# Query tiles in three buffers, a block's two averages in one place, and products in single PSUM banks, in a two-layer linear-attention kernel on one core

## The chip, the cores and the metric

The kernel runs on one NeuronCore of a Trainium2 chip. A core has TensorE (PE in the profile; its weight loads are PEld), VectorE (DVE), ScalarE (ACT), GpSimd (POOL) and SyncE (SP, which here issues the DMAs). Each takes its own instructions in order, and they wait for each other through semaphores. Matmuls write PSUM, which ScalarE and VectorE read. PSUM has eight banks; a tile of 512 float32 columns on 128 partitions fills one.

The metric is the device time of one execution in microseconds, the median of several. What matters for a change of well under one per cent is the median beside the spread of the runs.

## The reference

There are two layers with the same weights, and each is an attention half and a dense half. With S = 2048 rows, D = 640, H = 32 heads of Dh = 20 and F = 1536:

```python
q, k, v = split(layernorm(x) @ wqkv)                 # per head, Dh = 20
phi_q = concat([softmax(q @ w_phi), softmax(-(q @ w_phi))])   # 2 * Dh features
phi_k = concat([softmax(k @ w_phi), softmax(-(k @ w_phi))])
kv = phi_k^T v ;  z = sum over rows of phi_k         # over all S rows
o  = (phi_q kv) / (phi_q z + 1e-6)
x  = x + o @ wo
x  = x + mish(layernorm(x) @ w1 + b1) @ w2
```

The sums `kv` and `z` run over all rows. So no row's average `o` can be formed until the last key has been summed.

## The kernel before

**Tiling.** The 2048 rows are eight blocks (`NB`) of 256 rows, each two tiles (`BT`) of 128. All products of activations and weights are done as three matmuls in a split format: a high part by a high part, high by low, low by high. A product of 640 input columns therefore takes 5 x 3 = 15 matmuls for one half of the output columns (`project_half`, L354), and 30 for both (`project`). Transposed input comes as three pieces per block, of 2, 2 and 1 chunks of 128 columns; ScalarE makes the high part of each (`xth`) and VectorE the low part (`xtl`, L296).

**First stage of attention, `attend_first`.** For each block the kernel projects keys, values and queries of both tiles, in the order k0 k1 v0 v1 q0 q1 in most blocks. `features` then turns a projected tile into 1280 features: ScalarE copies the two PSUM halves into an SBUF tile `e` of 128 x 1280 (through the helper at L122), VectorE takes maxima and minima (L384) and the differences (L385, L387; for queries GpSimd does L385), ScalarE does the exponential, VectorE the sums (L393) and reciprocals (L394), GpSimd the product (L395). A key tile is then multiplied with the values into the running sum `kva` (L430), both tiles of a block one after the other, during the next block. A query tile is transposed in place by VectorE (L439) and stored by four DMAs (L443) to the DRAM tensor `e_d` of its block.

The tile `e` of a key is a `big_tile`, a pool with five buffers. The tile of query `i` is `query_tile(i)` (L368): one of two fixed SBUF tiles, `r210` and `r211` (both shown as `r` in the profile), that hold weights in the dense half. The PSUM pairs that the projections use are `mm_tile`, two buffers of two banks each. The other four banks are `one_tile`, four buffers of one bank each.

In this stage a scheduler orders each engine's instructions. In layer 0 it starts behind the folding of weights, in layer 1 behind the last steps of the dense half.

**Second stage, `attend_second`.** For TensorE and SP the order is the one that is written down. `load(b)` reads a block's query features back, transposed: two big tiles (L548) and a small one (L549). `load(0)` is called in the last block of the first stage; `load(1)` is called behind the last products of that stage, `load(2)` and `load(3)` after the averages that precede the block loop, and `load(b + 3)` inside it. `average(b, t)` multiplies the features of tile t with the block-diagonal sums `kvb` (L589, 44 matmuls as the trace counts them) into an `mm_tile`. VectorE divides by the denominators with five operations (L598, L599, L602) into a row tile. The division is `div[0]`, behind which `tail()` places one more step of what is left over from the first stage (`rest`: the second query tile of the last block, and the stores of that block's queries).

In each block b of the loop, the rows of block b are multiplied with `wo` (`Rows.half`, 15 matmuls each for two tiles and two column halves). VectorE adds each product to the residual (L619) and takes statistics (L620, L624). Between them stand the averages of block b + 1 and its transposes (L290, ten as the trace counts them). The second tile's two products go into the two banks of one `mm_tile`, `py`; the first tile's go into one bank each. SP's issues in a block are the next rows of x (L400), `load(b + 3)`, the store of the block (L671) and weights for the dense half (L147).

The dense half that follows (L697, L739) is not touched.

Of the kernel before, what the change touches and what calls it, by code (L numbers as in the profile page):

```python
# [8 lines left out]
F32 = mybir.dt.float32  # L9
# [17 lines left out]
NB = S // BLK  # L27
# [21 lines left out]
def kernel(  # L49
# [22 lines left out]
    def mm_tile():  # L72
        return psum.tile([P, 2, 512], F32, tag="mm", name="mm", bufs=2)

    def one_tile():
        return psum.tile([P, 512], F32, tag="one", name="one", bufs=4)

    def big_tile():
        return work.tile([P, EW], F32, tag="big", name="big", bufs=5)
# [7 lines left out]
    def row_block(t, b):  # L87
        return t[b * BLK:(b + 1) * BLK, :].rearrange("(p t) d -> p t d", t=BT)
# [75 lines left out]
    def r2_wide(j, dtype=F32R):  # L164
        return wts.tile([P, 2, D], dtype, tag=f"r2{j}", name=f"r2{j}")
# [140 lines left out]
    def row_tile():  # L306
        return work.tile([P, D], F32, tag="xn", name="xn", bufs=4)
# [40 lines left out]
    def project_half(ps, xts, t, ws, col, c, ks=range(KD), w=HC):  # L348
        sl = slice(t * P, (t + 1) * P)
        cs = slice(col + c * w, col + (c + 1) * w)  # L350
        for k in ks:
            h, l, wh, wl = xts.hs[k], xts.ls[k], ws[k][0][:, cs], ws[k][1][:, cs]
            for n, (a, r) in enumerate(((h, wh), (h, wl), (l, wh))):
                nc.tensor.matmul(ps[:, :w], a[:, sl], r, start=(k == 0 and n == 0),  # L354
                                 stop=(k == KD - 1 and n == 2))
# [9 lines left out]
        return g % 4, 2 * DH * (3 * (g // 4) + j)  # L365

    def query_tile(i):
        return r2_wide(10 + i % 2, F32).rearrange("p s d -> p (s d)")  # L368

    def features(ps, e, pool_sub):  # L370

# [26 lines left out]
    def fetch(x_src, b, xt=None):  # L398
        xt = x_tile() if xt is None else xt
        nc.sync.dma_start(xt, row_block(x_src, b))  # L400
        return xt
# [139 lines left out]
    def load(b):  # L541

        ta, tb, tc_ = big_tile(), big_tile(), pair_tile(F32)
        for t, g0 in ((ta, 0), (tb, 5)):

            src = e_d[b][120 * g0:120 * (g0 + 4) + P]
            src = bass.AP(tensor=src.tensor, offset=src.offset, ap=[[BLK, P], [120 * BLK, 5], [1, BLK]])
            nc.sync.dma_start(t.rearrange("f (g s) -> f g s", s=BLK), src)  # L548
        nc.sync.dma_start(tc_[:80, 0], e_d[b][1200:])  # L549
        return [(ta, tb)[g // 5][:, (g % 5) * BLK:(g % 5 + 1) * BLK] for g in range(10)] + [tc_[:, 0]]  # L550

    def finish_kv(kva):

        acc = row_tile()
        nc.vector.tensor_copy(acc[:, :360], kva[:, :360])
        yield
        ps = one_tile().rearrange("p (n q c) -> p n q c", n=4, c=32)
        for n in range(3):
            nc.tensor.transpose(ps[:120, n], acc[:, 120 * n:120 * (n + 1)], ident)
        for n, q, r, w in ((0, 4, 120, 3), (1, 4, 120, 3), (2, 2, 120, 3), (2, 1, 80, 2)):  # L560
            g = 4 * n + (2 if w == 2 else 0)
            q0 = 2 if w == 2 else 0
            nc.vector.tensor_tensor(
                kvb[:r, g:g + q, :(DH + 1) * w].rearrange("f q (j c) -> f q j c", j=w),
                ps[:r, n, q0:q0 + q, :DH + 1].unsqueeze(2).to_broadcast([r, q, w, DH + 1]),
                mask[:r, :w].unsqueeze(1).unsqueeze(3).to_broadcast([r, q, w, DH + 1]), op=ALU.mult)
        yield

    def attend_second(x_src, x_dst, acc, fetches, makes, fetch_next, begin_next):
        kva, o_ws, loaded, rest = acc  # L570
        rows = {}
        div = [None]

        def tail():

            with tc.issue_after(div[0]):
                next(rest, None)

        def average(b, t):

            phs = loaded[b]
            po = mm_tile()
            for g in range(G):
                n = 120 if g < 10 else 80
                w = GW if g < 10 else 42
                c, j = divmod(g, 8)
                for q in range(2):
                    s0 = t * P + 64 * q
                    nc.tensor.matmul(  # L589
                        po[64 * q:64 * q + 64, c, GW * j:GW * j + w], phs[g][:n, s0:s0 + 64],  # L590
                        kvb[:n, g, :w], start=True, stop=True)
            o = row_tile()
            den = work.tile([P, H], F32, tag="r", name="den", bufs=2)
            pv = [po[:, c, :(DH + 1) * n].rearrange("p (h d) -> p h d", d=DH + 1)
                  for c, n in ((0, 24), (1, 8))]
            hh = (slice(0, 24), slice(24, H))
            for c in range(2):
                nc.vector.tensor_scalar_add(den[:, hh[c]], pv[c][:, :, DH], DEN_EPS)  # L598
            nc.vector.reciprocal(den, den)  # L599
            for c in range(2):  # L600
                n = hh[c].stop - hh[c].start
                ins = nc.vector.tensor_tensor(o.rearrange("p (h d) -> p h d", d=DH)[:, hh[c]], pv[c][:, :, :DH],  # L602
                                        den[:, hh[c]].unsqueeze(2).to_broadcast([P, n, DH]), op=ALU.mult)
                div[0] = ins.ins
            rows.setdefault(b, []).append(o)
            if t == BT - 1:
                del loaded[b]

        class Rows:


            def __init__(self, b, t):
                self.t, self.xt, self.ps = t, xs[b], None
                self.bn = work.tile([P, 2, 6], F32, tag="bn", name="bn", bufs=2)

            def half(self, c, ps):
                project_half(ps, cur, self.t, o_ws, 0, c)
                part = self.xt[:, self.t, c * HC:(c + 1) * HC]
                nc.vector.tensor_tensor(part, ps[:, :HC], part, op=ALU.add)  # L619
                nc.vector.bn_stats(self.bn[:, c], part)  # L620

            def mean(self):
                mv = work.tile([P, 2], F32, tag="mv", name="mv", bufs=3)
                nc.vector.bn_aggr(mv, self.bn)  # L624
                return mv

        with tc.manual_schedule(engines={mybir.EngineType.PE, mybir.EngineType.SP}):
            kv = finish_kv(kva)
            next(rest)
            next(kv)  # L630
            loaded[1] = load(1)
            xs = {0: fetch(x_src, 0)}
            fetches[0]()
            next(rest)
            next(kv)
            next(rest)
            average(0, 0)
            average(0, 1)
            loaded[2] = load(2)
            average(1, 0)  # L640
            cur = Transposed(rows.pop(0)).all()
            average(1, 1)
            loaded[3] = load(3)
            for b in range(NB):
                if b == NB - 1:
                    ahead.all()
                elif b:
                    average(b + 1, 0)
                r0, r1 = Rows(b, 0), Rows(b, 1)
                r0.half(0, one_tile())  # L650
                if 0 < b < NB - 1:
                    average(b + 1, 1)
                tail()
                if b + 1 < NB:
                    xs[b + 1] = fetch(x_src, b + 1)
                if 0 < b and b + 3 < NB:
                    loaded[b + 3] = load(b + 3)
                if b == NB - 3:
                    fetch_next()
                r0.half(1, one_tile())  # L660
                mv0 = r0.mean()
                if b == NB - 2:
                    ahead = begin_next()
                py = mm_tile()
                r1.half(0, py[:, 0])
                if b + 1 < NB:
                    nxt = Transposed(rows.pop(b + 1)).all()
                r1.half(1, py[:, 1])
                norm_scale(b, [mv0, r1.mean()])
                xt = xs.pop(b)  # L670
                nc.sync.dma_start(row_block(x_dst, b), xt)  # L671
                makes[b]()
                if b + 1 < NB:
                    fetches[b + 1]()
                tail()
                if b < NB - 1:
                    cur = nxt
            for _ in rest:
                pass
        return ahead  # L680
# [217 lines left out]
```

## Time and profile before

| | |
|---|---|
| runs | 1399.83, 1400.14, 1402.13 us |
| median | 1400.14 us |
| the profiled execution | 1399.85 us, of which the span of the trace is 1397.9 us |
| mean granted TensorE clock | 0.994 |
| TensorE busy | 1364.9 us, 98% of the span |
| VectorE, ScalarE, GpSimd busy | 1089.6, 587.7 and 460.1 us |
| attention, layer 0 | about 18 to 350 us |
| attention, layer 1 | about 715 to 1055 us |

A row of the timeline gives start, duration, engine, line, operation, what it writes and reads, its size, how many such instructions were merged, and in brackets the idle time of the engine before it with what ended it. A row of the waits gives who waited for whom, the total in us, the number of waits and the longest. `L354` is line 354 of the kernel. Buffer numbers are left out of tile names, so `big` is any of the five big buffers, and `r` is either query tile (and the small tile of sums).

### The profile page before, as it was taken

The page shows a single profiled execution, that of the slowest core. Times are in us where ns is not written, and L with a number is a line of the kernel's source. Part 1 is how long each engine was busy: PE and PEld are TensorE (multiplying, and loading weights), DVE is VectorE, ACT ScalarE, POOL GpSimd, SP SyncE. Part 2 cuts the span into 40 slices and gives each one's busy share as a digit, 9 for nine tenths or more (in the row PEclk, how much of TensorE's full clock was granted, in tenths as well). Part 3 has the DMA queues.
Part 4 walks back from the last instruction along what each step waited for, and adds up shares of the span by engine and source line. Part 5 has one row for each costly group of instructions (what it writes and reads, how often), then busy time and mean ns, then how long its engine had stood idle before and what let it go on. Part 6 is the DMA issues. An engine that isn't in the chain of part 4 may idle for free. (4 is left out here: it accounts for less than half of the span.)

```text
span 1397.9 us, 30903 instructions
## 1 busy us (share of the span) xinstructions
PE 1364.9 (98%) x12866; PEld 1345.4 (96%) x12866; DVE 1089.6 (78%) x1814; ACT 587.7 (42%) x1035; POOL 460.1 (33%) x344
## 2 busy tenths in 40 slices
PE   7999999999999999999999999999999999999998
PEld 7989999999999999999999999989999999999998
DVE  5798877886688887788769899988667766777775
ACT  4444434222445454545443343432134544444443
POOL 1443543353442222222234544453344211211112
PEclk9999999999999999999999999999999999999999
DMA  8532434788624432344472433458965212333200
GB/s 312 156 60 63 88 51 93 201 242 290 207 62 95 114 96 65 73 107 104 137 229 56 91 67 58 67 118 268 279 236 177 74 26 71 95 95 95 68 28 20
DMA packets 350277, 169.03 MB, mean 121 GB/s; under 512 B 287097, under 2 KB 323689, under 8 KB 350137
## 3 DMA queue, kind: packets, MB, share of 16 engines
q1 hardware_dynamic: 350137, 167.06, 44.4%
q8 instruction: 101, 1.65, 0.5%
q14 instruction: 39, 0.32, 0.1%
HBM read 104.43 MB, written 62.59 MB: 119 GB/s over the span
## 5 line engine op out<-in xcount | busy, mean ns | idle before, releaser
L739 PE MATMUL mm<-r2h,ol 128*128 128x320 f32 x1280 | 305.4, 309 | 1.4 <-ACT ol L722 0.9
L723 POOL TENSOR_TENSOR ol<-big,ol 128x512 fp32r<-128x512 f32 (+1 forms) x98 | 130.6, 1333 | 458.1 <-ACT ol L722 393.0
L697 PE MATMUL one<-xtl,r1h 128*128 128x256 f32 x960 | 268.6, 280 | 2.0 <-DVE xtl L296 2.0
L697 PE MATMUL one<-xth,r1l 128*128 128x256 f32 x960 | 268.0, 279 | 0.0
L697 PE MATMUL one<-xth,r1h 128*128 128x256 f32 x960 | 266.5, 279 | 0.0
L739 PEld LDWEIGHTS mm<-r2h,ol 128*128 128x128 f32 x1280 | 219.1, 188 | 2.8 <-POOL ol L723 1.5
L739 PE MATMUL mm<-r2l,ol 128*128 128x320 f32 x640 | 197.3, 309 | 0.0
L354 PE MATMUL mm<-r1h,xth 128*128 128x304 f32 (+1 forms) x600 | 186.7, 311 | 6.8 <-ACT r L122 6.8
L354 PE MATMUL mm<-r1h,xtl 128*128 128x304 f32 (+1 forms) x600 | 185.4, 309 | 2.3 <-DVE xtl L296 2.2
L354 PE MATMUL mm<-r1l,xth 128*128 128x304 f32 (+1 forms) x600 | 185.5, 309 | 0.0
L697 PEld LDWEIGHTS one<-xtl,r1h 128*128 128x128 f32 x960 | 180.4, 188 | 2.7 <-DVE xtl L296 2.5
L697 PEld LDWEIGHTS one<-xth,r1l 128*128 128x128 f32 x960 | 180.4, 188 | 0.0
L697 PEld LDWEIGHTS one<-xth,r1h 128*128 128x128 f32 x960 | 179.9, 188 | 0.0
L712 DVE TENSOR_SCALAR big<-big 128x512 f32<-128x512 f32 (+1 forms) x98 | 56.6, 578 | 112.9 <-ACT big L710 112.9
L354 PE MATMUL mm<-r2h,xth 128*128 128x304 f32 (+1 forms) x460 | 142.6, 310 | 0.0
L354 PE MATMUL mm<-r2h,xtl 128*128 128x304 f32 (+1 forms) x460 | 140.4, 305 | 0.0
L354 PE MATMUL mm<-r2l,xth 128*128 128x304 f32 (+1 forms) x460 | 140.2, 305 | 0.0
L395 POOL TENSOR_TENSOR r<-r,r 128x1280 f32<-128x1280 f32 x32 | 77.5, 2423 | 149.0 <-DVE r L394 126.7
L354 PEld LDWEIGHTS mm<-r1h,xth 128*128 128x128 f32 x600 | 114.0, 190 | 8.1 <-ACT r L122 7.3
L710 ACT ACTIVATE big<-one,b1s 128x256 f32<-128x256 f32 x192 | 80.6, 468 | 96.2 <-PE one L697 95.6
L714 ACT ACTIVATE big<-big,two 128x512 f32<-128x512 f32 (+1 forms) x98 | 70.1, 715 | 119.2 <-DVE big L713 116.7
L739 PEld LDWEIGHTS mm<-r2l,ol 128*128 128x128 f32 x640 | 120.2, 188 | 0.0
(130 smaller groups left out, 3031.6 us busy)
## 6 DMA issues: line engine op xcount, KB each, us to landing
e_d<-r SPq DMA_DIRECT2D x128, 160.0 KB, 4.0
big<-e_d SPq DMA_DIRECT2D x32, 640.0 KB, 7.3
x_d<-xt SPq DMA_DIRECT2D x23, 640.0 KB, 4.0
xt<-x_d SPq DMA_DIRECT2D x22, 640.0 KB, 4.9
n_d<-xn SPq DMA_DIRECT2D x176, 80.0 KB, 2.4
xt<-in_x SPq DMA_DIRECT2D x16, 640.0 KB, 5.1
xn<-x_d SPq DMA_DIRECT2D x28, 320.0 KB, 4.2
v<-n_d SPq DMA_DIRECT2D x30, 256.0 KB, 3.2
```

What stands on the lines that cost most here:

```text
L354: nc.tensor.matmul(ps[:, :w], a[:, sl], r, start=(k == 0 and n == 0), stop=(k == KD - 1 and n == 2))
L395: nc.gpsimd.tensor_tensor(eg, eg, r.unsqueeze(2).to_broadcast([P, 2 * H, DH]), op=ALU.mult)
L697: nc.tensor.matmul(ph[:, j, :], l, r, start=(n == 0), stop=(n == 3 * KD - 1))
L710: exps[0] = nc.scalar.activation(part(ta, 0)[:, j - js.start], ph[:, j, :], AF.Exp, bias=b1s[:, 2 * pr + j:2 * pr + j + 1]).ins
L712: nc.vector.tensor_scalar_min(e, e, E_CAP)
L714: nc.scalar.activation(r, n, AF.Ln, bias=two)
L723: nc.gpsimd.tensor_tensor(al[:, js], n, ah[:, js].bitcast(F32), op=ALU.subtract)
L739: nc.tensor.matmul(pys[t][:, c, :HC], l[:, j, sl], r, start=(f == 0 and n == 0), stop=(f == KF - 1 and n == 2))
```

## The change

Three edits, all in the attention half.

```diff
     def query_tile(i):
-        return r2_wide(10 + i % 2, F32).rearrange("p s d -> p (s d)")
+        return big_tile() if i % 3 == 2 else r2_wide(10 + i % 3, F32).rearrange("p s d -> p (s d)")
```

Queries 0, 3, 6, 9, 12 and 15 use `r210`, queries 1, 4, 7, 10 and 13 use `r211`, and queries 2, 5, 8, 11 and 14 take one of the five buffers of the pool that keys and loads use. The number of big buffers stays five.

```diff
                 elif b:
                     average(b + 1, 0)
+                    average(b + 1, 1)
                 r0, r1 = Rows(b, 0), Rows(b, 1)
                 r0.half(0, one_tile())
-                if 0 < b < NB - 1:
-                    average(b + 1, 1)
                 tail()
```

In blocks 1 to 6 the second tile's average moves ahead of the first product with `wo`. `tail()` stays behind that product.

```diff
-                py = mm_tile()
-                r1.half(0, py[:, 0])
+                r1.half(0, one_tile())
                 if b + 1 < NB:
                     nxt = Transposed(rows.pop(b + 1)).all()
-                r1.half(1, py[:, 1])
+                r1.half(1, one_tile())
```

In every block the second tile's two products each take a single bank from the four. A block's turns in those banks become seven (four products, three transposes) instead of five, and its turns in the pairs two instead of three.

## The prediction

> **What bounds the kernel now.** I read the page first, then who waits for whom on TensorE, then the same question for ScalarE and VectorE in layer 1's first attention stage (735 to 945 us), and last the granted clock around TensorE's long waits.
>
> ```profile
> span 1397.9 us, 30903 instructions
> PE 1364.9 (98%) x12866; PEld 1345.4 (96%) x12866; DVE 1089.6 (78%) x1814; ACT 587.7 (42%) x1035; POOL 460.1 (33%) x344
> ```
> ```profile
> PE mm L354 <- ACT r L122: 6.8, 2, 3.8
> PE mm L589 <- PE mm L589: 0.9, 2, 0.4
> ```
> ```profile
> ACT r L122 <- DMA e_d<-r: 54.5, 12, 8.9
> DVE m L384 <- ACT r L122: 14.0, 7, 3.1
> ```
>
> TensorE is busy for 1364.9 of 1397.9 us, so an edit is worth what it removes from the 33 us that are left, or what it saves between matmuls. TensorE's largest wait is 6.8 us in two pieces: a projection needs a PSUM pair that ScalarE has not emptied. The fifth row says why: ScalarE cannot copy a query product into its SBUF tile, because that tile's predecessor is still being stored to `e_d`, 54.5 us of waiting in 12 pieces. VectorE in turn idles 14.0 us for those copies (775 to 945 us).
>
> ```profile
> 89.74 0.68 ACT L122 ACTIVATE r<-mm 128x608 f32<-128x608 f32 x1 [10.14 <-DMA e_d<-r]
> 90.47 0.41 PE L354 MATMUL mm<-r1h,xth 128*128 128x304 f32 x1 [3.03 <-ACT r L122]
> 770.00 0.68 ACT L122 ACTIVATE r<-mm 128x608 f32<-128x608 f32 x1 [8.91 <-DMA e_d<-r]
> 770.73 0.54 PE L354 MATMUL mm<-r1h,xth 128*128 128x304 f32 x1 [3.77 <-ACT r L122]
> 858.39 0.41 PE L354 MATMUL mm<-r1h,xtl 128*128 128x304 f32 x1 [1.83 <-DVE xtl L296]
> ```
> ```profile
> 770.85:774.26 3.41, 3.41 (x14) 3.41 (x15) 2.48 (x3) 0.25 (x1) 3.41 (x2) 0.50 0.92 143
> 856.18:859.59 3.41, 1.58 (x11) 1.33 (x10) 2.15 (x3) 0.32 (x1) 3.29 (x2) 1.00 0.85 145
> 859.60:863.01 3.41, 3.41 (x82) 3.11 (x84) 2.88 (x4) 1.33 (x4) 1.27 (x1) 0.50 0.23 79
> ```
> ```profile
> 961.86 2.20 PE mm L354 x15
> ```
>
> In the stretches (start:end, length, busy time of PE, PEld, DVE, ACT and POOL, granted clock, DMA share, GB/s) the clock is 0.50 for 3.41 us after such a wait. In one of them TensorE starts 14 matmuls; at full clock 15 take 2.20 us, about 0.145 each, so 3.41 us would fit 23 or 24. Each drop thus costs some 1.4 us on top of its wait. A wait of 1.83 us has already brought one on.
>
> **First edit: a third query tile.** With three buffers the copy of query i waits for the store of query i-3 instead of i-2. It is worth something different at each place.
>
> *Layer 0, at 90 us.* Query 3's tile becomes that of query 0, stored long before, so ScalarE's 10.14 us go. But VectorE is full here (61.8 of 63 us):
>
> ```profile
> 51.40:114.40 63.00, 59.97 (x643) 58.26 (x642) 61.84 (x75) 29.31 (x48) 30.84 (x21) 0.97 0.37 77
> ```
> ```profile
> 87.71 0.76 DVE L387 TENSOR_TENSOR big<-m,big 128x640 f32<-128x640 f32 x1
> 91.16 1.47 DVE L384 TENSOR_REDUCE m<-r 128x32 f32<-128x640 f32 x2
> ```
> ```profile
> 90.43 1.26 ACT L122 ACTIVATE big<-big 128x1280 f32<-128x1280 f32 x1
> 91.60 0.37 ACT L122 ACTIVATE xth<-one 128x256 fp32r<-128x256 f32 x1
> ```
>
> In the changed program's order query 3's reductions (1.47 us) stand ahead of the key's subtraction (87.71, 0.76 us), and ScalarE does that key's exponential (1.26 us) before the next block's last transposed piece (0.37 us). So the subtraction ends near 87.7 + 1.5 + 0.8 = 90.0, the exponential near 91.2, the piece near 91.6. TensorE starts that block at 87.4 (90.47 less the wait), runs the 12 matmuls that need no such piece, and waits from 89.1 to 91.6: 2.5 us, and the clock drops again. What is left is a head start of 12 matmuls (1.7 us) less what the key sums, split differently behind it, take of that: I take **0.4 us**, near the low end, because VectorE's row is full; bounds 0 and 3.03 + 1.4 = 4.4.
>
> *Layer 1, at 770 us.* Query 2 is copied at once, but VectorE is late with the next block's low parts:
>
> ```profile
> 767.90 0.62 DVE L296 TENSOR_TENSOR xtl<-xn,xth 128x512 fp32r<-128x512 f32 x1
> 770.86 1.55 DVE L384 TENSOR_REDUCE m<-r 128x32 f32<-128x640 f32 x2 [1.88 <-ACT r L122]
> 772.33 1.02 DVE L296 TENSOR_TENSOR xtl<-xn,xth 128x256 fp32r<-128x256 f32 x1
> ```
>
> The key projection can start at 767.0 (770.73 less the wait). It waits some 0.5 us for the second low part (ends 768.5) and 1.5 to 2 us for the third, which stands behind a reciprocal (0.5 us) and the reductions (1.55) and itself takes up to 1.02 us: 771 to 771.5. By the row at 858 that drops the clock too. The projection's end moves from 776.5 to about 775: **1.5 us**; bounds 0 and 3.77 + 1.4 = 5.2.
>
> *Layer 1, at 858 us.* The low part that TensorE lacks stands on VectorE behind a query's reductions, which wait for the query's copy, which waits for a store. Here VectorE has room:
>
> ```profile
> 776.00:942.00 166.00, 160.91 (x1882) 158.24 (x1884) 151.31 (x159) 64.68 (x110) 75.01 (x37) 0.99 0.41 77
> ```
>
> It is busy 151.3 of 166 us, and nearly all of the rest is the 14.0 us for the copies. The stall goes with its drop: 1.83 + 1.4 = **3.2 us**; bounds 0 and 3.2.
>
> *Layer 1, the key sums that end the stage.*
>
> ```profile
> ACT r L122 <- DMA e_d<-r: 8.4, 2, 4.5
> ```
> ```profile
> 260.12 1.48 PE L430 MATMUL one<-big,v 128*21 128x40 f32 x128 [0.68 <-POOL big L395]
> 941.08 2.26 PE L430 MATMUL one<-big,v 128*21 128x40 f32 x128 [3.18 <-POOL big L395]
> 916.89 0.82 DVE L384 TENSOR_REDUCE m<-r 128x32 f32<-128x640 f32 x1 [2.16 <-ACT r L122]
> ```
>
> In layer 0 (first row, 110 to 262 us) only two copies wait for stores, and the sums wait 0.68 us. In layer 1 they wait 3.18 us with a dropped clock, at the end of work that VectorE began 2.16 us late at 916.89, for a query's copy. I expect layer 0's wait: 2.5 + 1.4 = **3.9 us**; bounds 0 and 4.6.
>
> By the Trainium skill (TensorE: Matmul & The Clock Gate, "What's actually happening") the clock falls only after an idle window of about 3.4 us; by that the split waits at 90 and 770 us would keep it, and those two terms would come out at 1.8 and 2.9 us. The trace differs: 1.83 us of idle time in the window that ends at 859.59 was enough.
>
> **Its price in the big buffers.** The five now also hold queries 2, 5, 8, 11 and 14.
>
> ```profile
> 736.96 0.66 ACT L122 ACTIVATE r<-mm 128x608 f32<-128x608 f32 x1
> ```
> ```profile
> 230.65 9.71 SPq L548 DMA_DIRECT2D big<-e_d  x3
> 261.02 0.38 SPq L548 DMA_DIRECT2D big<-e_d  x1
> ```
> ```profile
> 267.36 0.80 PE L589 MATMUL mm<-kvb,big 120*64 120x63 f32 x20 [0.43 <-PE mm L589]
> 268.41 0.80 PE L589 MATMUL mm<-kvb,big 120*64 120x63 f32 x20 [0.24 <-DMA big<-e_d]
> ```
> ```profile
> 266.90:270.30 3.40, 2.72 (x56) 2.54 (x54) 2.64 (x11) 0.37 (x1) 0.00 (x0) 1.00 1.03 378
> ```
>
> Six blocks fill the 166 us above, 27.7 us each; eight tiles in three blocks leave each 52 us. A query needs 33 (copied at 736.96, stored by 770.00), a key about as long. No price there. It comes at the end of the stage: query 14 holds a fifth buffer until its last store, so `load(1)` has no free buffer and waits for the last keys' sums. Before, three halves of the first two loads were issued from 230.65 on; the fourth, issued at 261.02, landed at 268.4, just in time. Now the third goes at about 261.0 and the fourth when the sums end, at 261.6. Behind them on SP stand the rest of the load, x, a weight and the next load, all needed several us later. The DMA engines are full (share 1.03), so 640 KB more at 378 GB/s are 1.7 us. Block 1's first average begins at 268.4 instead of 267.36 and its second half between 269.2 and 270.1 instead of 268.41: 0.8 to 1.7 us, plus about a third of a chance of a drop. I take **+1.8 us per layer, +3.6**; bounds per layer 0 (layer 1 had slack) and 6, if the second half is 4.5 us late and the clock drops.
>
> **Second edit: averages together.** 44 matmuls (L589) move ahead of 15, in blocks 1 to 6 of each layer, with five VectorE operations and no DMA.
>
> ```profile
> 946.70 2.72 PE mm L589 x88
> ...
> 964.06 1.41 PE mm L589 x44
> 965.47 2.40 PE one L354 x15
> ...
> 973.89 1.09 PE one L290 x10
> ...
> 977.18 1.41 PE mm L589 x44
> ```
>
> 15 matmuls behind an average take 2.40 us, elsewhere 2.20. The block is 977.18 - 964.06 = 13.12 us; together it is 2.72 + 2.40 + 3 x 2.20 + 1.09 = 12.81. Twelve times 0.31 = **3.7 us**; bounds 0 and 3.7. The first product's addition on VectorE comes 1.4 us later; its bank is next needed two products on.
>
> **Third edit: single banks.** No matmul changes, and the pair that it frees has no waiter inside the blocks (the 0.9 us lie ahead of them). The last product reuses the third one's bank, emptied by L619 while ten transposes run (1.09 us):
>
> ```profile
> 987.04 0.49 DVE L619 TENSOR_TENSOR xt<-mm,xt 128x320 f32<-128x320 f32 x1 [0.94 <-PE mm L354]
> ```
>
> That leaves 0.6 us of cover. If L619 came late by one more 0.5 us operation, nothing would show; by two, some 0.4 us in 14 places, 5.6. VectorE was waiting here, so I take 0.
>
> **The sum.** -0.4 - 1.5 - 3.2 - 3.9 + 3.6 - 3.7 = -9.1 us on the profiled execution's own 1399.85 us (span 1397.9), 0.3 below the median of 1400.14: **1391 us**, own range 1386 to 1396.
>
> **Rivals.**
> *The waits vanish altogether.* For it: the copies' wait is the named releaser in every case. Against: VectorE is full at both early places. With the clock kept at 90 and 770 us and at the loads: -1.8 - 2.9 - 3.2 - 3.9 - 3.7 + 2.6 = -12.9, **1387**; with every upper bound and no price, 1379. The skill's clock rule points here.
> *VectorE stays behind.* The stalls at 858 and 941 us come back with VectorE as releaser. For it: 91% busy. Against: its 14.0 us of idle time. -0.4 - 1.5 - 3.7 + 3.6 = -2.0, **1398**.
> *The late load decides, slower.* Both halves of `load(1)` queue in the full DMA stretch, land 4.5 us late and drop the clock, 6 us per layer, with VectorE behind as well: -5.6 + 12 = +6.4, **1406**. It decides from 2.8 us per layer on. For it: share 1.03 and 0.24 us of slack; against: the full stretch moves 640 KB in 1.7 us.
> *The third tile changes nothing*, the store of query i-3 being late too: -3.7 + 3.6, **1400**.
>
> **How the numbers follow.** Forecast 0.50, waits vanish 0.17, VectorE behind 0.18, late load 0.12, nothing 0.03. A measurement tells 0.2% (2.8 us) from no change; a third of "VectorE behind" gets that far. Faster 0.72, same 0.16, slower 0.12. The range, 1382 to 1401, leaves out the late load and the far end of the first rival.
>
> **What would show it.** Right: no TensorE wait on ScalarE's `r`; short waits on transposed pieces near 89 and 768 us in their place; none near 855; layer 1's key sums waiting under 1 us; L589 in groups of 88 of some 2.7 us; 1 to 2 us of DMA wait at block 1's first average. Wrong: key copies waiting for a big buffer, or a load wait above 3 us.

## The result and the profile after

The changed kernel takes 1388.55 us, median of four runs (1387.53 to 1390.38), against 1399.99 us (1398.67 to 1402.13) for the kernel before on the same chip. The ratio is 0.9918, with a 95% interval of 0.99 to 0.9936: faster, as forecast, and 2.4 us below the 1391 of the forecast. The profiled execution took 1389.55 us.

The page of the changed kernel, span and engines:

```profile
span 1387.5 us, 30850 instructions
PE 1359.7 (98%) x12866; PEld 1342.9 (97%) x12866; DVE 1080.9 (78%) x1814; ACT 587.3 (42%) x1035; POOL 461.0 (33%) x344
```

Who waits for whom on TensorE in the changed kernel (total us, number, longest):

```profile
PE mm L354 <- DVE xtl L296: 3.0, 4, 1.4
PE mm L354 <- ACT xth L122: 2.7, 1, 2.7
...
PE mm L589 <- DMA big<-e_d: 1.1, 1, 1.1
```

The largest row of before, 6.8 us on ScalarE's `r`, is gone. The same view for ScalarE (735 to 945 us) and for VectorE (770 to 940 us):

```profile
ACT r L122 <- DMA e_d<-r: 6.0, 1, 6.0
```
```profile
DVE m L384 <- ACT r L122: 2.6, 3, 0.9
```

Of ScalarE's 54.5 us of waiting for stores 6.0 are left, of VectorE's 14.0 us for query copies (775 to 945 us) 2.6. So the third tile took the copies' waits away. TensorE's waits that remain, from the timeline of the changed kernel:

```profile
91.99 0.48 PE L354 MATMUL mm<-r1h,xth 128*128 128x304 f32 x1 [2.66 <-ACT xth L122]
...
94.13 0.62 PE L354 MATMUL mm<-r1h,xtl 128*128 128x304 f32 x1 [0.74 <-DVE xtl L296]
...
269.08 0.80 PE L589 MATMUL mm<-kvb,big 120*64 120x63 f32 x20 [0.43 <-DVE xn L602]
270.98 0.80 PE L589 MATMUL mm<-kvb,big 120*64 120x63 f32 x20 [1.10 <-DMA big<-e_d]
...
769.05 0.41 PE L354 MATMUL mm<-r1h,xtl 128*128 128x304 f32 x1 [0.51 <-DVE xtl L296]
...
771.55 0.62 PE L354 MATMUL mm<-r1h,xtl 128*128 128x304 f32 x1 [1.39 <-DVE xtl L296]
...
933.36 1.48 PE L430 MATMUL one<-big,v 128*21 128x40 f32 x128 [0.94 <-POOL big L395]
```

Nothing waits near 855 us. Layer 1's key sums wait 0.94 us instead of 3.18. The waits at 92 and 770 us changed their releaser: ScalarE's and VectorE's own order in place of a store. Around them, in stretches of the granted clock (start:end, length, busy time of PE, PEld, DVE, ACT and POOL, granted clock, DMA share, GB/s):

```profile
88.77:92.18 3.41, 0.75 (x6) 0.50 (x5) 3.41 (x4) 1.78 (x3) 3.41 (x2) 1.00 0.09 25
92.19:95.60 3.41, 2.67 (x38) 2.19 (x38) 3.38 (x7) 0.50 (x2) 2.78 (x2) 0.50 0.00 0
95.60:99.01 3.41, 3.41 (x43) 3.11 (x44) 1.91 (x2) 0.42 (x1) 2.73 (x2) 0.50 0.15 25
768.03:771.44 3.41, 1.62 (x10) 1.12 (x8) 3.41 (x7) 0.83 (x2) 2.84 (x2) 1.00 0.92 143
771.44:774.85 3.41, 3.30 (x13) 3.30 (x14) 3.41 (x4) 0.00 (x0) 3.41 (x2) 0.50 0.88 154
```

In layer 0 the clock is at half for two windows now, where it was one; at 771 us still for one; at 860 and 941 us no longer.

The averages stand together (timeline of the changed kernel; 40 and 4 matmuls are one average):

```profile
952.17 1.25 PE L290 MATMUL one<-ident,xn 128*128 128x128 f32 x10
...
955.55 1.38 PE L589 MATMUL mm<-kvb,big 120*64 120x63 f32 x40
...
958.25 0.42 PE L354 MATMUL one<-r2h,xth 128*128 128x320 f32 x1
...
990.53 1.25 PE L290 MATMUL one<-ident,xn 128*128 128x128 f32 x10
```

Both take 2.70 us (955.55 to 958.25), and three blocks 38.36 us (952.17 to 990.53): 12.79 each, where before a block took 13.12.

Four stretches sort the gain and all the experiments: A from layer 0's first key sums (L430) to its last group of them, B from there to the third contraction of the dense half (its 49th matmul of L739 before, L737 after; 11.3 us behind the first in every run), C and D the same in layer 1. "Half" is the time at half clock ahead of the last few us. A to D and "half" are of one profiled execution, the median is of all runs.

| kernel | A | B | C | D | half | median us |
|---|---|---|---|---|---|---|
| before | 183.87 | 136.94 | 189.33 | 138.02 | 13.7 | 1400.1 |
| changed | 185.37 | 135.79 | 181.14 | 135.27 | 10.2 | 1388.55 |
| changed, again (e8) | 185.22 | 135.54 | 180.37 | 134.97 | 6.8 | 1388.48 (one run) |
| e1 third tile alone | 185.93 | 138.34 | 180.37 | 138.16 | 6.8 | 1394.39 |
| e2 averages alone | 182.20 | 135.47 | 189.73 | 136.65 | 10.2 | 1397.05 |
| e3 banks alone | 183.67 | 136.48 | 189.52 | 138.83 | 13.7 | 1399.20 |
| e4 third tile in layer 1 | 182.18 | 134.47 | 180.36 | 136.26 | 0 | 1385.27 |
| e5 query 14 apart | 184.96 | 134.50 | 181.19 | 135.77 | 10.2 | 1388.02 |
| e6 early piece | 179.87 | 135.54 | 181.29 | 135.66 | 0 | 1384.45 |
| e7 = e5 + e6 | 179.87 | 134.47 | 181.33 | 135.59 | 0 | 1383.78 |
| e9 early in layer 0 | 179.86 | 134.47 | 180.38 | 135.94 | 0 | 1382.78 |
| e10 early in both | 179.98 | 134.60 | 179.82 | 134.78 | 0 | 1381.35 |

The whole gain of the change lies in C (-8.2), D (-2.75) and B (-1.15). A became longer by 1.5 us.

### The profile page after: what moved, and what is told of

Its sections match the earlier page's. It is cut to its first block, busy times and chain, and to the rows that moved or that the text cites. A ratio compares the mean times of both kernels' runs of the same rounds, so it can differ in the third digit from the quotient of the medians.

```text
span 1387.5 us, 30850 instructions
## 1 busy us (share of the span) xinstructions
PE 1359.7 (98%) x12866; PEld 1342.9 (97%) x12866; DVE 1080.9 (78%) x1814; ACT 587.3 (42%) x1035; POOL 461.0 (33%) x344
## 4 chain that ended last, share of the span: by engine, by line
PE 80%; DVE 7%; DMA 2%; ACT 1%; issue 1%; POOL 1%; DVEq 0%; ACTq 0%; POOLq 0%; SPq 0%
PE one L695 22%; PE mm L737 21%; PE mm L354 20%; PE one L354 11%; PE mm L589 3%; PE one L290 2%; PE one L430 1%; DVE m L384 1%; DVE r L393 1%; DVE xtl L296 1%; DVE big L710 1%; DVE big L717 1%; DMA big<-e_d 1%; DVE r L439 1%; DVE big L711 0%
## 5 line engine op out<-in xcount | busy, mean ns | idle before, releaser
L737 PE MATMUL mm<-r2h,ol 128*128 128x320 f32 x1280 | 305.4, 310 | 1.5 <-ACT ol L720 0.9
L737 PEld LDWEIGHTS mm<-r2h,ol 128*128 128x128 f32 x1280 | 219.2, 188 | 2.8 <-POOL ol L721 1.5
L737 PE MATMUL mm<-r2l,ol 128*128 128x320 f32 x640 | 197.4, 309 | 0.0
L395 POOL TENSOR_TENSOR big<-big,r 128x1280 f32<-128x1280 f32 x42 | 102.7, 2444 | 82.5 <-DVE r L394 66.6
L737 PEld LDWEIGHTS mm<-r2l,ol 128*128 128x128 f32 x640 | 120.3, 188 | 0.0
L354 PEld LDWEIGHTS mm<-r1h,xtl 128*128 128x128 f32 x600 | 114.3, 191 | 4.0 <-DVE xtl L296 4.0
L720 ACT ACTIVATE ol<-big 128x512 fp32r<-128x512 f32 (+1 forms) x98 | 61.0, 622 | 131.4 <-DVE big L719 131.3
L354 PEld LDWEIGHTS mm<-r1l,xth 128*128 128x128 f32 x600 | 114.2, 190 | 0.2
```

The source lines that it names most:

```text
L395: nc.gpsimd.tensor_tensor(eg, eg, r.unsqueeze(2).to_broadcast([P, 2 * H, DH]), op=ALU.mult)
L720: nc.scalar.activation(ah[:, js], n, AF.Copy)
L737: nc.tensor.matmul(pys[t][:, c, :HC], l[:, j, sl], r, start=(f == 0 and n == 0), stop=(f == KF - 1 and n == 2))
```

## Experiments

All edits are on the changed kernel unless "before" is named. The kernel before ran beside each group of them, at 1400.1 us.

### e1, e2, e3: the three edits one at a time (on the kernel before)

```diff
# e1
-        return r2_wide(10 + i % 2, F32)...
+        return big_tile() if i % 3 == 2 else r2_wide(10 + i % 3, F32)...
# e2
                     average(b + 1, 0)
+                    average(b + 1, 1)
...
-                if 0 < b < NB - 1:
-                    average(b + 1, 1)
# e3
-                py = mm_tile()
-                r1.half(0, py[:, 0])
+                r1.half(0, one_tile())
...
-                r1.half(1, py[:, 1])
+                r1.half(1, one_tile())
```

> The kernel before with the third query tile alone. Theory (the waits for the stores were the larger part, the averages the smaller, and the two add up): the change's 11.4 us less 12 x 0.33 for the averages leaves -7.4 us on 1400.0, 1392.6; no TensorE wait on ScalarE's r, layer 1's key sums near 933.5 us, blocks of the second stage still 13.1 us each. Rival (the gain of layer 1 needs the averages or the banks too, which leave the pair free earlier): -4 us or less, 1396 to 1400. Rival (the third tile is all of it): -11, 1389.

Measured: 1394.39 us, ratio 0.996 (0.9947 to 0.9972), -5.7 us. The theory holds for C, which is as short as with all three edits (180.37), and for the waits on `r`, which are gone. It was 1.8 us too hopeful. Two of TensorE's three waits for `e_d` (timeline of e1) show where:

```profile
269.82 0.80 PE L589 MATMUL mm<-kvb,big 120*64 120x63 f32 x20 [1.18 <-DMA big<-e_d]
...
271.53 0.80 PE L589 MATMUL mm<-kvb,big 120*64 120x63 f32 x20 [0.91 <-DMA big<-e_d]
```

2.09 us where the kernel before waited 0.43 + 0.24. B is 1.4 us longer than before. So the third tile is about half of the gain, and the rival that it is all of it falls.

> The kernel before with a block's two averages in one place, second tile's products still in a pair. Theory: 12 blocks of about 12.79 instead of 13.12 us, -4.0 us on 1400.0, 1396.0; first stages as before. Rival (the averages' saving needs the single banks, since average, average and product pair take turns in two pairs): 0 to -1 us, 1399 to 1400, with waits of TensorE on VectorE's additions (L619) ahead of L589 or L354.

Measured: 1397.05 us, ratio 0.9978 (0.997 to 0.9987), -3.1 us, between the two. Blocks 1 and 2 of the loop take 13.32 and 13.15 us, the other four 12.79, in both layers. TensorE's waits in e2, 270 to 395 us, and the two places in its timeline:

```profile
PE mm L589 <- DVE xt L619: 0.5, 2, 0.3
```
```profile
281.40 0.80 PE L589 MATMUL mm<-kvb,big 120*64 120x63 f32 x20 [0.33 <-DVE xt L619]
...
294.55 0.63 PE L589 MATMUL mm<-kvb,big 120*64 120x63 f32 x14 [0.17 <-DVE xt L619]
```

An average needs the pair that the second tile's products have just filled, and VectorE has not emptied it. That costs 0.53 + 0.36 = 0.9 us a layer, 1.8 in all; why blocks 3 to 6 don't wait stays open. So the second edit is worth its 0.33 us in every block only with the third. A is 1.7 us shorter than before, which is not the edit's: e3 and e2 both wait 2.85 us for the store near 90 us (the kernel before 3.03), but in e2 no half clock follows (windows of e3, then of e2):

```profile
87.63:91.04 3.41, 1.26 (x9) 1.26 (x10) 3.41 (x5) 1.99 (x4) 2.72 (x2) 1.00 0.22 43
91.04:94.45 3.41, 3.41 (x65) 3.00 (x65) 3.38 (x6) 1.00 (x3) 3.41 (x2) 0.50 0.00 0
```
```profile
88.16:91.57 3.41, 1.63 (x11) 1.63 (x12) 3.41 (x5) 2.36 (x5) 2.72 (x2) 1.00 0.08 24
```

A of e3 and A of e2 (183.67 and 182.20) thus price one window of half clock at 1.5 us; the forecast had 1.4.

> The kernel before with the second tile's products in single banks alone. Theory: no difference beyond 0.5 us, 1400; blocks still 13.12 us. Rival (the last product waits for L619's addition to empty the third one's bank): +0.4 us in 14 places, 1405.6. Rival (the pair was a hidden wait): blocks shorter by 0.1 us and more, 1398 or less.

Measured: 1399.2 us, ratio 0.9995 (0.9986 to 1.0004): no difference. Blocks take 13.12 us. Both rivals fall. Alone the banks are worth nothing; they keep the averages' gain whole.

### e4: the third tile in layer 1 only

```diff
-        return big_tile() if i % 3 == 2 else r2_wide(10 + i % 3, F32)...
+        if layer:
+            return big_tile() if i % 3 == 2 else r2_wide(10 + i % 3, F32)...
+        return r2_wide(10 + i % 2, F32)...
```

> The changed kernel with the third query tile in layer 1 only; layer 0 takes turns in two as before. Theory (in layer 0 the third tile only moves the wait at 90 us to VectorE and ScalarE, two windows of half clock instead of one, and its big buffer delays the first load): 1.7 us less in layer 0's first stage and 0.8 us less at its load, 1386.0 against 1388.5 for the change. Rival (the double clock drop comes from something else, or waits in layer 0 later on take the place): 1388 to 1389. Rival (layer 0 gains from the third tile between 100 and 260 us, hidden by the drop): 1390 and above.

Measured: 1385.27 us (1384.87 to 1385.63), ratio 0.9899 (0.9884 to 0.9914). It is 3.3 us faster than the change, more than the 2.5 of the theory; the runs of the two don't overlap. A is 3.2 us shorter than in the change's first trace, B 1.3; D, with a wait of 1.59 us for `e_d`, is 1.0 longer. So in layer 0 the third tile costs time. Part of A's difference is another matter: the window at half clock that the kernel before and e3 have near 90 us, some 1.5 us by e2 and e3, is missing in e4, as the timeline and the windows of e4 show:

```profile
90.27 0.41 PE L354 MATMUL mm<-r1h,xth 128*128 128x304 f32 x1 [2.82 <-ACT r L122]
```
```profile
88.73:92.14 3.41, 1.87 (x13) 1.87 (x14) 3.41 (x5) 2.60 (x5) 2.71 (x2) 1.00 0.09 24
92.15:95.56 3.41, 3.41 (x78) 2.99 (x77) 3.38 (x5) 0.38 (x2) 3.31 (x3) 1.00 0.02 5
764.57:767.98 3.41, 2.01 (x13) 1.76 (x14) 3.41 (x6) 0.83 (x2) 3.41 (x3) 1.00 0.93 144
767.98:771.39 3.41, 3.41 (x27) 3.41 (x25) 3.04 (x2) 1.16 (x3) 3.41 (x3) 1.00 0.72 174
```

The wait for the store is back, 2.82 us, and yet no window is at half clock: it fell across two windows, and in the one that ends at 92.14 TensorE was busy for 1.87 us. The 0.52 and 1.40 us near 766 us did not bring half clock on here either.

### e8: the changed kernel once more

> The changed kernel once more, for another execution's clock rows. Theory (the clock is judged in a grid of windows of 3.41 us that lies differently over each execution: a window with TensorE busy less than about 0.48 of it is followed by one at half clock, one with 0.48 or more by full clock): the same waits at 92 and 771 us as in the first trace, but half clock behind them only where the new grid leaves a window under 0.48; with 1.90 us of idle time in two pieces at 769 to 771 most grids would not. Rival (a wait of that length always brings half clock on): rows at 0.5 at 92 and 771 us again, of 6.83 and 3.41 us.

Measured: 1388.48 us. The waits in its timeline are those of the first trace; the windows are not:

```profile
769.01 0.41 PE L354 MATMUL mm<-r1h,xtl 128*128 128x304 f32 x1 [0.51 <-DVE xtl L296]
...
771.50 0.41 PE L354 MATMUL mm<-r1h,xtl 128*128 128x304 f32 x1 [1.39 <-DVE xtl L296]
```
```profile
87.93:91.34 3.41, 0.86 (x7) 0.61 (x5) 3.41 (x4) 1.49 (x3) 3.41 (x2) 1.00 0.11 25
91.34:94.75 3.41, 2.71 (x36) 2.23 (x37) 3.41 (x6) 0.80 (x3) 2.78 (x2) 0.50 0.00 0
...
767.18:770.59 3.41, 2.42 (x16) 1.93 (x14) 3.41 (x6) 0.19 (x1) 2.04 (x1) 1.00 0.94 147
770.60:774.01 3.41, 2.51 (x18) 2.51 (x19) 3.41 (x5) 0.63 (x2) 3.41 (x3) 1.00 0.85 135
```

With the same 1.90 us of idle time, the first execution had nearly all of it in one window (1.62 us busy) and got half clock; this one had it in two (2.42 and 2.51) and did not. From the end of the wait to the second key sums it takes 4.68 us (771.50 to 776.18), the first execution 6.14 (771.55 to 777.69): half clock cost 1.46 us there. C is only 0.77 us shorter, since from the second to the third key sums this execution takes 25.65 us against 24.97, with a wait of 0.41 us at 799.40 that the first one doesn't have. The theory holds, and the rival falls for the place at 770 us. At 92 us the 3.2 to 3.7 us of waiting in two pieces brought two windows of half clock in all four executions that had it (the change twice, e1, e5).

### e5: query 14 apart from the big buffers

Query 14 takes the tile of query 12, and query 15 that of query 13.

```diff
-        return big_tile() if i % 3 == 2 else r2_wide(10 + i % 3, F32)...
+        return big_tile() if i % 3 == 2 and i < 14 else r2_wide(10 + (i % 3 if i < 14 else i % 2), F32)...
```

> The changed kernel with query 14 in the tile of query 12 instead of a big buffer, so that the first load finds free buffers before the last keys' sums. Theory (the held buffer is what makes TensorE wait 1.53 us for e_d at layer 0's first averages, and was worth about nothing in layer 1): the wait for e_d goes, 0.5 to 1.5 us less than the change's 1388.6, 1387.5. Rival (query 14 then waits for query 12's store, VectorE for query 14, and the last keys' sums of layer 1 for VectorE, as before the change): their wait is 2 to 3 us instead of 0.94, with a slow clock behind it in some executions, 1389.5 to 1391.

Measured: 1388.02 us (1386.95 to 1392.4), ratio 0.9919 (0.9904 to 0.9934). The times alone don't settle it; the trace does. At layer 0's first averages no wait for `e_d` is left, and B falls from 135.79 to 134.50. Layer 1's last key sums wait 0.95 us, so the rival falls. D isn't shorter (135.77). This execution's window ahead of 769 us is the border case; at 1.69 us, 0.495 of the window, it lies above the 0.48 of e8's theory and is followed by half clock all the same:

```profile
765.90:769.31 3.41, 1.69 (x10) 1.45 (x11) 3.41 (x6) 0.83 (x2) 3.41 (x2) 1.00 0.91 139
769.31:772.72 3.41, 3.41 (x15) 3.41 (x14) 3.41 (x3) 0.01 (x1) 3.41 (x3) 0.50 0.86 150
```

### e6, e7: the last piece of block 2 earlier

```diff
-                    elif n > 2:
+                    elif n > 2 and len(nxt.hs) < KD:
                         nxt.step()
+                        if b == 1 and n == 4:
+                            nxt.step()
```

e7 has e5's edit too.

> The changed kernel with the last transposed piece of block 2 made one place earlier in block 1 (two pieces ahead of the second query's projection or the like place, none ahead of the last), in both layers. Theory (the waits left at 90 and 770 us are only the order on ScalarE and VectorE, a key's exponential and a query's reductions ahead of the last piece): the wait at 92 us falls from 3.4 us in two pieces to 1 us or less without a window of half clock, the 1.9 us near 770 to 0.5 or less: 3 to 6 us less than 1388.6, 1384. Rival (VectorE is full in layer 0's blocks 1 to 3, so what is moved ahead makes the keys late): the wait turns up behind block 2 as one of L430 or of an xtl, and the time stays at 1387 to 1389 or above.

> The two edits of e5 and e6 together, on the changed kernel. Theory: they add up, 1383 us. Rival (e5's edit brings layer 1's wait at the end of the stage back): 1385 to 1387.

Measured: e6 1384.45 us (1382.93 to 1384.64), ratio 0.9885 (0.9872 to 0.9897); e7 1383.78 us, ratio 0.9882 (0.9869 to 0.9895). The timeline of e6:

```profile
92.69 0.83 PE L430 MATMUL one<-big,v 128*21 128x40 f32 x64 [1.05 <-POOL big L395]
...
763.66 0.41 PE L354 MATMUL mm<-r1h,xtl 128*128 128x304 f32 x1 [0.52 <-DVE xtl L296]
...
766.15 0.41 PE L354 MATMUL mm<-r1h,xtl 128*128 128x304 f32 x1 [1.39 <-DVE xtl L296]
...
794.98 0.41 PE L354 MATMUL mm<-r1h,xtl 128*128 128x304 f32 x1 [1.34 <-DVE xtl L296]
```

In layer 0 the theory holds: of 3.4 us one wait of 1.05 is left, no window is at half clock, and A is 5.5 us shorter than in the change. So the wait at 92 us was the order on ScalarE and VectorE. The 1.05 us on a key is the wait that the rival foretold, but the time is the theory's. In layer 1 the theory failed: both waits stay, and a third of 1.34 us joins them. e7 takes B down by 1.07 us more, as e5 did; its layer 1 has the same three waits.

### e9, e10: layer 0 alone, and layer 1 another way

```diff
# e9: as e7, but
-                        if b == 1 and n == 4:
+                        if b == 1 and n == 4 and layer == 0:
# e10: as e9, and
                         nxt = xt if layer else normed(b + 1, xt)
+                        if b == 1 and layer:
+                            nxt.step()
```

> As e7, but the last piece earlier in layer 0 only; layer 1 makes its pieces as before. Theory (in layer 1 the early piece did nothing at 766 us and brought a wait of 1.34 us in place of 0.41 near 795 us): 0.9 us less than e7's 1383.8, 1382.9. Rival (the two waits are not tied to it): 1383.8.

> As e9, and in layer 1's block 1 each of the three pieces of block 2 one place earlier (at the third, fourth and fifth of its six products; they need no TensorE work there). Theory (the wait of 0.52 and 1.39 us near 766 us is the order of VectorE alone, and VectorE has room in layer 1): both gone, 1.9 us less, 1381.0, and no window of half clock there in any execution. Rival (VectorE is full there too: what the pieces are moved ahead of comes late): a wait of 1 to 2 us on another tile between 766 and 800 us, 1382.5 to 1384.

Measured: e9 1382.78 us (1381.81 to 1384.12), ratio 0.9868 (0.985 to 0.9886), with C 0.95 us shorter than in e7: the theory's number, and the wait near 794 us is 0.43 instead of 1.38 us. The intervals of e7 and e9 overlap; what shows it is the trace. e10 1381.35 us (1379.99 to 1383.73), ratio 0.9862 (0.9845 to 0.9879). The time is the theory's, the reason only in part. From the timeline of e10:

```profile
769.23 0.97 PE L430 MATMUL one<-big,v 128*21 128x40 f32 x81 [0.43 <-POOL big L395]
...
792.93 0.41 PE L354 MATMUL mm<-r1h,xtl 128*128 128x304 f32 x1 [1.20 <-DVE xtl L296]
```

The 1.9 us near 766 us are gone, but a block later TensorE waits 1.20 us where e9 waited 0.43: the rival's turn. C gains 0.56 us, not 1.9. The rest is in D, where a wait of 1.22 us at an average is gone that comes and goes from kernel to kernel (see the loads below). It can't be credited to the edit. e10 has the lowest median of all: some 7 us below the change, 19 below the kernel before. The intervals of e9 and e10 overlap.

## Why the prediction was right, step by step

**What bounds it.** Right. The copies' wait for stores was the cause in layer 1: with the third tile alone C falls from 189.33 to 180.37 us, and the other two edits do nothing to it (189.73, 189.52).

**Layer 0 at 90 us: forecast -0.4, measured +1.5,** outside the bounds of 0 to 4.4 us of gain. This is the step that failed. The order of the operations was right, and so was the first piece: 2.5 us forecast, 2.66 measured. Missed was the piece's low part, the next thing that is late. VectorE in the changed kernel:

```profile
90.23 2.38 DVE L272 SCALAR_TENSOR_TENSOR stats<-mv,stats 128x1 f32<-128x1 f32 x2
92.53 0.54 DVE L394 RECIPROCAL r<-r 128x64 f32<-128x64 f32 x1
93.00 0.75 DVE L387 TENSOR_TENSOR r<-m,r 128x640 f32<-128x640 f32 x1
93.67 0.40 DVE L296 TENSOR_TENSOR xtl<-one,xth 128x256 fp32r<-128x256 f32 x1
```

Two statistics, a reciprocal and the query's subtraction stand ahead of it. So TensorE waits 0.74 us more at 94.13, inside the window of half clock, and the next window is at half clock too. I took the work that is moved ahead of the key's exponential and didn't follow it to the piece behind. In sum TensorE idles 3.40 us there instead of 3.03, so the waits take back the whole head start of 12 matmuls, and the second window at half clock (some 1.5 us by e2 and e3) makes it a loss.

**Layer 1 at 770 us: forecast -1.5.** From layer 1's first key sums to its third, 52.09 us before (751.75 to 803.84), the changed kernel takes 50.44 (752.22 to 802.66), 1.65 less. The split into about 0.5 and 1.5 to 2 us was 0.51 and 1.39. Half clock came in the first execution and not in the second, which takes 0.8 us less still. Of the eight executions that had these two waits two had it (the change's first and e5): I had put as certain what came in two of eight.

**Layer 1 at 858 us: forecast -3.2.** Right in kind, and too small: from the fourth key sums to the fifth it takes 30.38 us before (831.38 to 861.76), 27.18 after, and the fifth group itself still ran at half clock before (timeline of the kernel before; in the changed kernel it starts at 857.05 and takes 1.48 us):

```profile
861.76 2.03 PE L430 MATMUL one<-big,v 128*21 128x40 f32 x128
```

From the group's start to the next projection it takes 1.96 us before and 1.40 after: that is the 0.56 us by which the stretch from the fifth to the sixth key sums is shorter. Together the place gave 3.8 us, above the bound of 3.2.

**Layer 1's key sums: forecast -3.9.** They wait 0.94 us, not the 0.68 of layer 0, without half clock: 2.2 us less of waiting (seventh key sums to eighth, 23.87 us before, 21.64 after) and 1.5 less from there to the first average (5.55 before, 4.04 after), 3.7.

**The loads: forecast +1.8 per layer.** In layer 0 the two late halves are issued at 262.74 and 263.35 us, the second lands at 270.93, and TensorE waits 0.43 + 1.10 us instead of 0.43 + 0.24: +0.9. Taking query 14 out of the pool gains 1.1 to 1.3 us (B: 135.79 to 134.50, and 135.54 to 134.47 from e6 to e7), so cause and place were right and the size was high. In layer 1 D's -2.75 and -3.05 leave 0.4 to 0.7 us for the term, beside 2.0 for the averages and 1.5 for the half clock. No wait of TensorE is put down to `e_d` there in either execution of the change, but one more wait stands at an average ahead of the block loop, in the change (timeline; 0.23 us in e8) and, longer, in e4 (waits):

```profile
944.75 0.68 PE L589 MATMUL mm<-kvb,big 120*64 120x63 f32 x16 [0.36 <-issue]
```
```profile
PE mm L591 <- DMA big<-e_d: 1.6, 1, 1.6
```

Such waits take 0.73 us in e6, 1.03 in e5, 0.85 in e7, 1.22 in e9, and none is listed in e10. D less these waits is 134.7 to 134.9 us in all eight executions that have the three edits in layer 1. So they are what varies in D, and it is not query 14, which is out of the pool in e5, e7, e9 and e10. In e4 and mostly in e6 the profile puts them down to the landing of a load; for the others it names no releaser, and why they come and go stays open.

**The averages: forecast -3.7; the banks: 0.** Twelve blocks by 0.33 us are 4.0: two averages in one place take 2.70 us instead of twice 1.41, and one group of 15 matmuls less stands behind an average (2.40 us instead of 2.20). The two terms are not independent, as I had them: without the banks 1.8 of the 4.0 are lost to the pair.

**What was left out.** Between the third and fourth, and between the sixth and seventh key sums of layer 1 the change saves another 0.33 and 0.22 us. There the kernel before starts a matmul on a low part (`xtl`) 0.38 us (828.94) and 0.27 us (914.78) after the one before it, and the next 0.25 us behind that, where 0.14 is usual. The changed kernel has no such pause. That these two low parts were late for the same copies, as at 858 us, is likely but not shown.

**The sum.** Against the forecast, layer 0 at 90 us is 1.9 us worse and the key sums 0.2. The loads are 2.0 us better in the first execution, 858 us 0.6, what was left out 0.55, the averages 0.3 and 770 us 0.15. That takes -9.1 to some -10.6; the four stretches together are 10.6 us shorter, and the span 10.4. The total was near because the wrong terms largely cancel, and that is luck. Of the rivals, "VectorE stays behind" fell: nothing waits near 855 us, and the key sums wait 0.94 us. "The late load decides" fell: it needed 2.8 us per layer, and the loads cost 0.9 and at most 0.7. "The third tile changes nothing" fell with e1. "The waits vanish altogether" gave 1387, nearer to the result than the forecast; its mechanism fell all the same, since the waits at 92 and 770 us are there.

## What to carry to other kernels

Where a buffer is added, follow the work that is now early to the next thing on its engine's queue, and the one behind that: a wait was taken from a store here and given to two pieces standing behind the query's work, in layer 0 at a loss. An edit that helps one stage needn't be made in all of them; layer 0 was better with two tiles, or with the late piece moved ahead. And where two edits share a resource (here the pairs of PSUM banks), they are not priced apart.

## What the runs showed of the hardware

The clock is judged in windows of 3.41 us: its stretches at half clock last 3.41 or 6.83 us. The grid of these windows lay differently over the two executions of the changed kernel (borders at 771.44 and 770.59 us, around waits that ended at 771.55 and 771.50). In twelve executions (before, the change and e1 to e10), behind the first 15 us and ahead of the last 15, each full-clock window in which TensorE was busy for 1.62 us or less was followed by one at half clock (fifteen, down to 0.12 us). One with 1.63 us (e2, ending at 91.57) was not, one with 1.69 (e5) was, and none with 1.82 or more was followed by one. The border lies near half a window, as far as the modelled ends of matmuls let it be seen.

So whether waits of 1.8 to 3 us bring half clock on depends on where they fall in the grid: 2.85 us did in e3 and not in e2, 2.82 us didn't in e4, and 1.90 us did in one execution of the change and not in the other. By the Trainium skill (TensorE: Matmul & The Clock Gate, "What's actually happening") the window is 3413 ns and free-running, which agrees. The Trainium skill also lists, in the same section, the idle state as coming after at least one idle window; here windows with up to 1.62 us of work, nearly half, were enough.

After a first window at half clock with 2.67 us of busy time another followed (2.71 in e8), while one that was full (3.41, the kernel before) ended it. In e2 a half-clock window with 2.49 us ended it too, so the rule for the way back isn't settled.
